# First layer of the later groups: 26 block products in four banks in place of 7 products in two

## The chip, the core and the metric

The kernel runs on one core of a Trainium2 chip. The metric is the device time of one execution in microseconds. The engines of the core are TensorE (in profiles PE for matmuls, PEld for its weight loads), VectorE (DVE), ScalarE (ACT), GpSimd (POOL) and SyncE (SP, which issues the transfers). Each engine works through its own list of instructions, and semaphores hold an instruction back until what it needs is there.

## The reference

An attention with decay (a "retention") over 4 batches, 8 heads, 768 positions and head size 64 gives x of 3072 tokens by 512. Two matmuls with an activation between them follow:

```python
def _moe_ref(x, w_in, w_out):
    h = x @ w_in                     # (3072, 512) @ (512, 2048)
    sp = np.maximum(h, 0.0) + np.log1p(np.exp(-np.abs(h)))
    g = h * erf(sp)
    return (g @ w_out).astype(np.float32)   # (3072, 2048) @ (2048, 512)
```

All is fp32 on the chip; the two weight matrices arrive as 64-bit floats and are converted on VectorE and ScalarE.

## The kernel before

The first 512 tokens go through plain matmuls while the weights are still being converted. The other 2560 tokens go in ten chunks of 256, and each chunk in two halves of the hidden columns (s = 0 and 1): 20 "later groups". In a later group both layers use Strassen's scheme in its form with seven products (Winograd): a 2x2 block product with sums of blocks takes 7 block products in place of 8. Here is the first layer:

```python
PRODUCTS = {
    1: ("11", "11"), 2: ("12", "21"), 3: ("S4", "22"), 4: ("22", "T4"),
    5: ("S1", "T1"), 6: ("S2", "T2"), 7: ("S3", "T3"),
}
...
def hidden_part(g, p):
    m, s = chunk_of(g), (g - G0) % 2
    ...
    a, b = PRODUCTS[p]
    if a[0] == "S":
        need("sums in", s)
    bank = BK[g][0 if p in (1, 6, 7, 4) else 1]
    for u in range(FG):                      # FG = 4
        for kk in range(2):
            nc.tensor.matmul(                # line 852
                bank[:, u, :],
                w_in_sb[:, s, IN[a], kk, u * P : (u + 1) * P],
                XS[m][b][:, kk, :],
                start=(p in (1, 2, 5) and u == 0 and kk == 0), stop=True, ...
            )
    pace(1.5)
    flat = bank.rearrange("p u t -> p (u t)")
    if p == 1:
        nc.scalar.copy(h["11"], flat)
    elif p == 2:
        nc.vector.tensor_tensor(h["11"], h["11"], flat, op=ALU.add)
    ...                                      # 4 copies and 3 additions in all, 128x512 each
```

So a group has 7 x 8 = 56 matmuls of 128x128x128. The sums S of the weights are made once per half by `sums`, four operations of 128x1024; the sums T of the inputs once per chunk by `x_sums`, four of 128x256. The order of a later group:

```python
for g in range(G0, NG):
    first = g == G0
    more = j < NJ
    hidden_part(g, 1)
    hidden_part(g, 2)
    if first:
        gated(g - 1)
    if put is not None:
        for step in range(3):
            put_part(put, step)
    hidden_part(g, 6)
    if first:
        sub_begin(j)
        sub_states(j)
    for _ in range(2):
        next(last_steps, None)
    ...
    if not first:
        g_sums(g - 1)
    hidden_part(g, 5)
    hidden_part(g, 7)
    for _ in range(2):
        next(last_steps, None)
    ...
        project_part(g - 1, 1)
    hidden_part(g, 4)
    hidden_part(g, 3)
    if more:
        sub_visit(j, g)                      # attention of one block of 128 positions
    if g + 1 < NG and (g - G0) % 2:
        x_sums(g + 1)
    if more:
        ... K_(j + 2); T(j + 2)              # scales and transposes on VectorE
    ...
        for p in (2, 4):
            project_part(g - 1, p)
        gate(g)                              # Softplus, then Erf, on ScalarE
        for p in (5, 6, 7, 3):
            project_part(g - 1, p)
    ...
        gated(g)                             # h * erf on VectorE, two of 128x1024
```

`last_steps` yields the sums for the second half of w_in and for w_out one operation at a time; `need` runs it until what is asked for is done. `project_part` is one product of the second layer (4 matmuls of 128x256), and ends with `next(last_steps, None)`; products 5, 6, 7 and 3 read the sums that `g_sums` makes, and 4 to 7 read sums of w_out ("T1" to "T4"). `put_part` adds the products of a chunk up to the output. PSUM has two banks from `ps_h` (hp), two from `ps_r` (r, also used by the attention) and four from `ps_o` (o).

The conversion of the weights uses scratch in places that are free early on: the parts of w_in_sb and w_out_sb that the sums will fill later.

Of the kernel before, what the change touches and what calls it, by code (L numbers as in the profile page):

```python
# [13 lines left out]
U32 = mybir.dt.uint32  # L14
# [18 lines left out]
IN = {"11": 0, "12": 1, "21": 2, "22": 3, "S3": 2, "S1": 4, "S2": 5, "S4": 6}  # L33
# [6 lines left out]


# [4 lines left out]
def kernel(  # L46
# [84 lines left out]
    w_in_sb = const.tile([P, 2, 7, 2, FG * P], F32, name="w_in_sb")  # L131
    w_out_sb = const.tile([P, 2, 7, FG, DH], F32, name="w_out_sb")

    def w_in_of(ft, kk):
        half, s, i = ft // (2 * FG), ft % (2 * FG) // FG, ft % FG
        return w_in_sb[:, s, 2 * half + kk // 2, kk % 2, i * P : (i + 1) * P]

    def w_out_of(ft):
# [6 lines left out]
    spare = [  # L145
        x[:, s, 4:7].rearrange("p a b c -> p (a b c)") for s, x in
        ((0, w_out_sb), (1, w_out_sb), (1, w_in_sb), (0, w_in_sb))
    ]
    raws = [x[:, : 2 * CE].bitcast(I64) for x in spare]
    numbers = spare[0][:, 2 * CE :].bitcast(U32)  # L150
    powers = [x[:, 2 * CE :].bitcast(U32) for x in spare[1:3]]
# [38 lines left out]
    def conversion(n):  # L190

        which, i = pieces[n]
        half, s, at = i // 4, i % 4 // 2, i % 2


        parts = itertools.product(
            range(2) if n < 4 else (None,), (slice(2), slice(2, 4)) if n == 0 else (slice(None),)
        )  # L200
        for part, rows in parts:
            last = n > 0 or rows.start == 2
            words = raws[place[n]].bitcast(U32)
            if which == "in":
                f = slice(at * 2 * P, (at + 1) * 2 * P)
                if part is not None:
                    f = slice((at * 2 + part) * P, (at * 2 + part + 1) * P)
                to = w_in_sb[:, s, 2 * half : 2 * half + 2, :, f].rearrange("p d k f -> p (d k) f")
            else:
                to = w_out_sb[:, s, 2 * half : 2 * half + 2, at * 2 : at * 2 + 2, :].rearrange(  # L210
                    "p d f c -> p d (f c)"
                )
            words = words.rearrange("p (a b w) -> p a b w", a=to.shape[1], w=2)
            number, power = (
                x.rearrange("p (a b) -> p a b", a=to.shape[1]) for x in (numbers, powers[n % 2])
            )
            if part is not None:
                f = slice(part * P, (part + 1) * P)
                words, number, power = words[:, rows, f], number[:, rows, f], power[:, rows, f]
                to = to[:, rows]  # L220
            lo, hi = words[:, :, :, 0], words[:, :, :, 1]
            nc.vector.tensor_scalar(power, hi, 0x7FF00000, None, op0=ALU.bitwise_and)
            nc.scalar.activation(power, power, AF.Relu, bias=below, scale=8.0)
            if part is None:
                yield
            nc.vector.tensor_scalar(
                number, hi, 0xFFFFF, 1 << 20, op0=ALU.bitwise_and, op1=ALU.bitwise_or
            )
            yield
            numberf = number.bitcast(F32)  # L230
            nc.vector.scalar_tensor_tensor(numberf, number, 2.0**32, lo, op0=ALU.mult, op1=ALU.add)
            if part is None:
                yield
            nc.vector.scalar_tensor_tensor(
                power, hi, 1 << 31, power, op0=ALU.bitwise_and, op1=ALU.bitwise_or
            )
            if part != 0 and last:
                load_pieces_after(n)
            yield
            nc.vector.scalar_tensor_tensor(  # L240
                to, numberf, 2.0**-52, power.bitcast(F32), op0=ALU.mult, op1=ALU.mult,
            )
            if last:
                done.update((which, 2 * i + u) for u in (range(2) if part is None else (part,)))
            yield

    def sums(which, s):

        if which == "in":
            assert all(("hidden", 2 * FG + s * FG + u) in done for u in range(FG))  # L250
            x = {name: w_in_sb[:, s, at] for name, at in IN.items()}
            of = (("S1", "21", "22", 1), ("S2", "S1", "11", 0), ("S3", "11", "21", 0), ("S4", "12", "S2", 0))
        else:
            assert ("project", s) in done
            x = {name: w_out_sb[:, s, at] for name, at in OUT.items()}
            of = (("T1", "12", "11", 0), ("T2", "22", "T1", 0), ("T3", "22", "12", 0), ("T4", "21", "T2", 0))
        for to, a, b, plus in of:
            nc.vector.tensor_tensor(x[to], x[a], x[b], op=ALU.add if plus else ALU.subtract)
            yield
        done.add(("sums " + which, s))  # L260
# [76 lines left out]
    state_1, state_2 = (const.tile([P, HP, D], F32, name=f"state{i}") for i in range(1, 3))  # L337
# [479 lines left out]
    XS, BK = {}, {}  # L817
# [6 lines left out]
    def x_quarter(m, dh, th):  # L824
        at = m % 2 * SCH + th * P
        return XC[m // 2][:, 2 * dh : 2 * dh + 2, at : at + P]

    def x_sums(g):

        m = chunk_of(g)  # L830
        xs = ret.tile([P, 4, 2, P], F32, name="xs", bufs=1)
        b11, b12, b21, b22 = (x_quarter(m, d, t) for d in range(2) for t in range(2))
        t1, t2, t3, t4 = (xs[:, i] for i in range(4))
        for to, a, b in ((t1, b12, b11), (t2, b22, t1), (t3, b22, b12), (t4, b21, t2)):
            nc.vector.tensor_tensor(to, a, b, op=ALU.subtract)
        XS[m] = {"11": b11, "21": b21, "22": b22, "T1": t1, "T2": t2, "T3": t3, "T4": t4}

    def hidden_part(g, p):


        m, s = chunk_of(g), (g - G0) % 2
        if p == 1:
            HS[g] = act.tile([P, N], F32, name="h")
            BK[g] = [ps_h.tile([P, FG, P], F32, name="hp") for _ in range(2)]
        h = {name: HS[g][:, i * TCH : (i + 1) * TCH] for name, i in HQ.items()}
        a, b = PRODUCTS[p]
        if a[0] == "S":
            need("sums in", s)
        bank = BK[g][0 if p in (1, 6, 7, 4) else 1]
        for u in range(FG):  # L850
            for kk in range(2):
                nc.tensor.matmul(  # L852
                    bank[:, u, :],
                    w_in_sb[:, s, IN[a], kk, u * P : (u + 1) * P],
                    XS[m][b][:, kk, :],
                    start=(p in (1, 2, 5) and u == 0 and kk == 0),
                    stop=True,
                    skip_group_check=True,
                )
        pace(1.5)  # L860
        flat = bank.rearrange("p u t -> p (u t)")
        if p == 1:
            nc.scalar.copy(h["11"], flat)
        elif p == 2:
            nc.vector.tensor_tensor(h["11"], h["11"], flat, op=ALU.add)  # L865
            pace(-0.6)
        elif p == 6:
            nc.scalar.copy(h["12"], flat)  # L868
        elif p == 7:
            nc.scalar.copy(h["22"], flat)  # L870
            other = BK[g][1].rearrange("p u t -> p (u t)")
            nc.vector.tensor_tensor(h["22"], h["22"], other, op=ALU.add)  # L872
            pace(-0.6)
        elif p == 4:
            nc.scalar.copy(h["21"], flat)  # L875
        elif p == 3:
            nc.vector.tensor_tensor(h["12"], h["12"], flat, op=ALU.add)  # L877
            pace(-0.6)
# [18 lines left out]
    def g_sums(g):  # L897
# [4 lines left out]
        for i in range(4):  # L902
            x[f"S{i + 1}"] = HS[g][:, i * TCH : (i + 1) * TCH]
        for to, a, b, plus in (
# [3 lines left out]
        G[g] = x  # L908
        pace(-2.4)
# [87 lines left out]
    def next_scores():  # L997
# [39 lines left out]
            ([], [(x_sums, G0)]),  # L1037
# [4 lines left out]
    for g in range(G0):  # L1042
# [10 lines left out]
        if g:  # L1053
            for tt in range(TT):
# [12 lines left out]
                elif g == G0 - 1 and tt == 1:  # L1067
                    load(JPC + 4)

    j = JPC + 2
    put = None
    for g in range(G0, NG):
        first = g == G0
        more = j < NJ
        hidden_part(g, 1)
        hidden_part(g, 2)
        if first:
            gated(g - 1)  # L1080
        if put is not None:
            for step in range(3):
                put_part(put, step)
        hidden_part(g, 6)
# [3 lines left out]
        for _ in range(2):  # L1088
            next(last_steps, None)
        if put is not None:  # L1090
            put_part(put, 3)
            put = None
        if not first:
            g_sums(g - 1)
        hidden_part(g, 5)
        hidden_part(g, 7)
        for _ in range(2):
            next(last_steps, None)
        if first:
            K_(j + 1)  # L1100
            T(j + 1)
            project(g - 1, 0)
        else:
            project_part(g - 1, 1)
        hidden_part(g, 4)
        hidden_part(g, 3)

# [17 lines left out]
        else:  # L1125
            for p in (2, 4):
                project_part(g - 1, p)
# [68 lines left out]
```

## Time and profile before

| | |
|---|---|
| time, median of 2 runs | 679.71 us (679.61 to 679.81) |
| span of the profiled execution | 677.6 us |
| TensorE busy | 671.8 us, 99% of the span |
| VectorE busy | 392.1 us, 58% |
| ScalarE busy | 257.0 us, 38% |
| mean granted TensorE clock | 1.000 |

Busy time is the time in which at least one instruction of the engine runs. In the list of groups a row has the line, the engine and operation, output and inputs with shapes, the count, the busy time and mean length of one, and the idle time of the engine just before such instructions with what ended it. Every fp32 matmul stands in the list as two records. A timeline row has the start in us from the span's start, the length, and the instruction; where rows overlap, operations are queued and the distance of their starts is what one of them costs.

### The profile page before, as it was taken

The page shows a single profiled execution, that of the slowest core. Times are in us where ns is not written, and L with a number is a line of the kernel's source. Part 1 is how long each engine was busy: PE and PEld are TensorE (multiplying, and loading weights), DVE is VectorE, ACT ScalarE, POOL GpSimd, SP SyncE. Part 2 cuts the span into 40 slices and gives each one's busy share as a digit, 9 for nine tenths or more (in the row PEclk, how much of TensorE's full clock was granted, in tenths as well). Part 3 has the DMA queues.
Part 4 walks back from the last instruction along what each step waited for, and adds up shares of the span by engine and source line. Part 5 has one row for each costly group of instructions (what it writes and reads, how often), then busy time and mean ns, then how long its engine had stood idle before and what let it go on. Part 6 is the DMA issues. An engine that isn't in the chain of part 4 may idle for free.

```text
span 677.6 us, 14849 instructions
## 1 busy us (share of the span) xinstructions
PE 671.8 (99%) x6400; PEld 575.4 (85%) x6400; DVE 392.1 (58%) x635; ACT 257.0 (38%) x294; POOL 7.4 (1%) x20
## 2 busy tenths in 40 slices
PE   8999999999999999999999999999999999999998
PEld 7744444668999999999999999999999999999997
DVE  5999999667845445634644553554554544333324
ACT  3477453333414415334144143242341441432430
POOL 1000000200000000000000000000000000000000
PEclk9999999999999999999999999999999999999999
DMA  9999753333423112312322321222222300000000
GB/s 188 231 254 256 178 144 77 59 61 62 119 48 75 34 32 47 76 36 43 76 41 38 76 46 31 64 44 47 69 40 45 74 2 1 1 33 1 1 32 31
DMA packets 156721, 47.67 MB, mean 70 GB/s; under 512 B 143088, under 2 KB 147568, under 8 KB 156656
## 3 DMA queue, kind: packets, MB, share of 16 engines
q1 hardware_dynamic: 156240, 46.72, 31.6%
q8 instruction: 50, 0.82, 0.5%
q14 instruction: 15, 0.12, 0.1%
q10 hardware_dynamic: 416, 0.01, 0.0%
HBM read 40.39 MB, written 6.29 MB: 69 GB/s over the span
## 4 chain that ended last, share of the span: by engine, by line
PE 98%; DMA 1%; DVE 0%; SPq 0%; ACT 0%; issue 0%
PE hp L852 37%; PE o L924 36%; PE hp L759 8%; PE o L795 8%; PE r L638 2%; PE hp L530 1%; PE o L674 1%; DMA kq<-in_k_dram 1%; PE hp L653 1%; PE r L459 1%; PE r L653 1%; PE o L506 1%; PE r L446 1%; PE r L674 0%; PE o L515 0%; PE o L499 0%
## 5 line engine op out<-in xcount | busy, mean ns | idle before, releaser
L852 PE MATMUL hp<-xs,w_in_sb 128*128 128x128 f32 x1280 | 149.7, 275 | 0.0
L852 PEld LDWEIGHTS hp<-xs,w_in_sb 128*128 128x128 f32 x1280 | 147.8, 192 | 1.5 <-issue 0.5
L924 PE MATMUL o<-w_out_sb,h 128*128 128x256 f32 (+1 forms) x648 | 142.0, 377 | 0.4 <-DVE r L1151 0.4
L924 PEld LDWEIGHTS o<-w_out_sb,h 128*128 128x128 f32 x648 | 122.3, 190 | 16.8 <-DVE r L1151 0.6
L852 PE MATMUL hp<-xT,w_in_sb 128*128 128x128 f32 x960 | 113.7, 275 | 0.0
L852 PEld LDWEIGHTS hp<-xT,w_in_sb 128*128 128x128 f32 x960 | 112.0, 192 | 1.9 <-issue 1.0
L924 PE MATMUL o<-w_out_sb,e 128*128 128x256 f32 x480 | 112.1, 383 | 0.0
L748 DVE TENSOR_TENSOR e<-h,e 128x1024 f32<-128x1024 f32 x42 | 49.5, 1221 | 100.0 <-ACT e L729 100.0
L924 PEld LDWEIGHTS o<-w_out_sb,e 128*128 128x128 f32 x480 | 88.3, 190 | 11.4
L759 PE MATMUL hp<-xT,w_in_sb 128*128 128x512 f32 (+2 forms) x144 | 56.5, 548 | 0.0
L877 DVE TENSOR_TENSOR h<-h,hp 128x512 f32<-128x512 f32 x20 | 13.8, 688 | 72.3 <-PE hp L852 72.3
L719 ACT ACT_TABLE_LOAD x24 | 30.8, 1283 | 60.8 <-issue 45.4
L759 PEld LDWEIGHTS hp<-xT,w_in_sb 128*128 128x128 f32 x144 | 25.8, 190 | 26.9 <-issue 24.6
L729 ACT ACTIVATE e<-e 128x2048 f32<-128x2048 f32 (+1 forms) x23 | 42.1, 1836 | 0.2
L719 ACT ACTIVATE e<-h 128x2048 f32<-128x2048 f32 x22 | 42.0, 1910 | 0.2
L865 DVE TENSOR_TENSOR h<-h,hp 128x512 f32<-128x512 f32 x20 | 13.7, 687 | 37.5 <-PE hp L852 37.5
L870 ACT COPY h<-hp 128x512 f32<-128x512 f32 x20 | 11.7, 586 | 61.0 <-PE hp L852 61.0
L875 ACT COPY h<-hp 128x512 f32<-128x512 f32 x20 | 11.7, 585 | 60.3 <-PE hp L852 60.3
L868 ACT COPY h<-hp 128x512 f32<-128x512 f32 x20 | 11.7, 585 | 57.1 <-PE hp L852 57.1
L692 ACT COPY xT<-r 128x256 f32<-128x256 f32 x33 | 10.8, 375 | 57.9 <-PE r L638 57.9
L729 ACT ACT_TABLE_LOAD x24 | 30.8, 1283 | 0.4
L872 DVE TENSOR_TENSOR h<-h,hp 128x512 f32<-128x512 f32 x20 | 13.8, 688 | 27.8 <-ACT h L870 27.8
(144 smaller groups left out, 667.8 us busy)
## 6 DMA issues: line engine op xcount, KB each, us to landing
w_out_sb<-in_moe_w_out_dram SPq DMA_DIRECT2D x14, 512.0 KB, 5.5
kq<-in_k_dram SPq DMA_DIRECT2D x23, 256.0 KB, 3.9
v<-in_v_dram SPq DMA_DIRECT2D x23, 256.0 KB, 3.2
out_dram<-r SPq DMA_DIRECT2D x23, 256.0 KB, 2.7
kq<-in_q_dram SPq DMA_DIRECT2D x288, 16.0 KB, 1.8
kb<-in_k_dram SPq DMA_DIRECT2D x288, 16.0 KB, 1.7
w_in_sb<-in_moe_w_in_dram SPq DMA_DIRECT2D x8, 512.0 KB, 9.5
w_in_sb<-in_moe_w_in_dram SPq DMA_DIRECT2D x8, 256.0 KB, 7.7
```

The source lines that it names most:

```text
L638: nc.tensor.matmul(pp[r][col * D : (col + 1) * D, u % 2, t], x[own, u, :], QT[j][own, u, t], start=first(r, col), stop=True, skip_group_ch ...
L653: nc.tensor.matmul(other[a][own, u % 2, D:] if crossed else pp[a][own, u % 2, t], V[j][t, 2 * u + r, :], AM[j][t, r, u, :D], start=crossed ...
L719: nc.scalar.activation(E[g], HS[g], AF.Softplus)
L729: nc.scalar.activation(E[g][:, half], E[g][:, half], AF.Erf)
L748: nc.vector.tensor_tensor(E[g][:, half], HS[g][:, half], E[g][:, half], op=ALU.mult)
L759: nc.tensor.matmul(HP_[ft][:, t], w_in_of(ft, kk), XC[0][:, kk, t], start=(kk == 0), stop=(kk == n_k - 1),)
L795: nc.tensor.matmul(O[0][tt].rearrange("p (d c) -> p d c", d=2), E[g][:, u * TCH + tt * P : u * TCH + (tt + 1) * P], w_out_of(ft), start=(f ...
L852: nc.tensor.matmul(bank[:, u, :], w_in_sb[:, s, IN[a], kk, u * P : (u + 1) * P], XS[m][b][:, kk, :], start=(p in (1, 2, 5) and u == 0 and ...
L865: nc.vector.tensor_tensor(h["11"], h["11"], flat, op=ALU.add)
L872: nc.vector.tensor_tensor(h["22"], h["22"], other, op=ALU.add)
L877: nc.vector.tensor_tensor(h["12"], h["12"], flat, op=ALU.add)
L924: nc.tensor.matmul(O[m][i][:, half, at], G[g][a][:, u * P : (u + 1) * P], w_out_sb[:, s, OUT[b], u, at], start=i not in started, stop=(s = ...
```

## The change

The first layer of a later group is cut finer: 4x4 blocks of weights times 4x2 blocks of inputs, 26 block products in place of 28 (7 products of 4 blocks each). Each product ("step") is two matmuls of 128x128x128 for 256 hidden columns. The steps are spread over four banks, two hp and two r. In each bank they form chains: a step mostly adds to what is there, and the running sum is read after the step, sometimes by two readers. The first read of each of the 8 blocks of h is a copy on ScalarE, the others are additions or subtractions on VectorE. The aim is fewer matmuls.

It needs other sums: 30 of the weights per half (128x256 each, many in place), 18 of the inputs per chunk (128x128 each). w_in_sb is laid out in 26 blocks, and the conversion's scratch moves: one part into the tile xs of the inputs' sums, one into a slice of w_out_sb; the state of the attention's third block goes into a buffer of kb. The core of the diff:

```diff
+N_W, N_X = 26, 18
+W_SUMS = (
+    (16, 2, 6, "+"),
+    (17, 8, 10, "-"),
+    ...                                      # 30 in all: target, operands, sign
+)
+X_SUMS = (
+    (0, (1, 0), (1, 1), "-"),
+    ...                                      # 18 in all
+)
+STEPS = (                                    # weight, input, bank, starts the chain, reads
+    (21, (1, 0), 0, True, ((4, True),)),
+    (20, 5, 1, True, ((1, False),)),
+    (10, 14, 2, True, ((3, True),)),
+    (22, 0, 3, True, ((5, True),)),
+    (23, 7, 0, False, ((5, True),)),
+    (24, (0, 1), 1, False, ((7, False),)),
+    (25, 15, 2, False, ((2, True),)),
+    (14, (2, 1), 3, False, ((7, True),)),
+    (9, 8, 0, False, ((7, True),)),
+    (12, 6, 1, False, ((6, False),)),
+    (2, 11, 2, True, ((2, False), (6, True))),
+    (17, 1, 3, True, ((2, False), (4, True))),
+    (15, 10, 0, False, ((6, True),)),
+    ...                                      # 26 in all
+)
...
-    w_in_sb = const.tile([P, 2, 7, 2, FG * P], F32, name="w_in_sb")
+    w_in_sb = const.tile([P, 2, N_W, 2 * P], F32, name="w_in_sb")
...
-    powers = [x[:, 2 * CE :].bitcast(U32) for x in spare[1:3]]
+    later = ret.tile([P, N_X, P], F32, name="xs", bufs=1)[:, : CE // P].rearrange("p a f -> p (a f)")
+    powers = [halves(spare[1][:, 2 * CE :]), halves(later)]
+    last_power = halves(spare[1][:, :CE])
...
+    def sum_in(s, upto):
+        while in_sums[s] < upto:
+            to, a, b, sign = (x if i == 3 else w_in_sb[:, s, x] for i, x in enumerate(W_SUMS[in_sums[s]]))
+            nc.vector.tensor_tensor(to, a, b, op=OP[sign])
+            in_sums[s] += 1
...
     def sums(which, s):
         if which == "in":
+            for n in range(4, 17, 4):
+                sum_in(s, n)
+                yield
+            return
...
-    def hidden_part(g, p):
+    def hidden_steps(g):
+        banks = [pool.tile([P, FG, P], F32, name=name) for pool, name in ((ps_h, "hp"), (ps_r, "r")) for _ in range(2)]
+        for w, x, bank, first, reads in STEPS:
+            sum_in(s, max([n for n, of in enumerate(W_SUMS, start=1) if of[0] == w], default=0))
+            to = banks[bank]
+            for u in range(2):
+                nc.tensor.matmul(
+                    to[:, u, :],
+                    w_in_sb[:, s, w, u * P : (u + 1) * P],
+                    XS[m](x),
+                    start=first and u == 0,
+                    ...
+            of = to[:, :2].rearrange("p u t -> p (u t)")
+            for o, plus in reads:
+                h = h_block(g, o)
+                if o in written:
+                    nc.vector.tensor_tensor(h, h, of, op=ALU.add if plus else ALU.subtract)
+                elif plus:
+                    nc.scalar.copy(h, of)
+                else:
+                    nc.scalar.activation(h, of, AF.Copy, scale=-1.0)
+                written.add(o)
+            yield
```

The order of a later group becomes:

```diff
-        hidden_part(g, 1)
-        hidden_part(g, 2)
...
-        for _ in range(2):
-            next(last_steps, None)
...
         if first:
             sub_begin(j)
             sub_states(j)
+        elif put is not None:
+            put_part(put, 0)
+        more_sums = iter(()) if first else g_sums(g - 1)
+        for n, _ in enumerate(hidden_steps(g), start=1):
+            if first:
+                if n == 2:
+                    gated(g - 1)
+                elif n == 14:
+                    K_(j + 1)
+                    T(j + 1)
+                    project(g - 1, 0)
+                continue
+            if n in (4, 5, 8) and put is not None:
+                put_part(put, {4: 1, 5: 2, 8: 3}[n])
+            if n in (13, 14, 15, 16):
+                next(more_sums)
+            if n in (14, 18, 24):
+                project_part(g - 1, {14: 1, 18: 2, 24: 4}[n])
...
-            for p in (2, 4):
-                project_part(g - 1, p)
             gate(g)
             for p in (5, 6, 7, 3):
                 project_part(g - 1, p)
```

Both calls of `next(last_steps, None)` outside `project_part` are gone, and the first `x_sums` moves behind the end of the conversion.

## The prediction

> **What bounds the kernel now.** I read the engines' busy shares first, then the chain that ended last, then the costliest groups of instructions.
>
> ```profile
> PE 671.8 (99%) x6400; PEld 575.4 (85%) x6400; DVE 392.1 (58%) x635; ACT 257.0 (38%) x294; POOL 7.4 (1%) x20
> ...
> PE 98%; DMA 1%; DVE 0%; SPq 0%; ACT 0%; issue 0%
> PE hp L852 37%; PE o L924 36%; PE hp L759 8%; PE o L795 8%; PE r L638 2%; PE hp L530 1%; PE o L674 1%; DMA kq<-in_k_dram 1%; PE hp L653 1%; PE r L459 1%; PE r L653 1%; PE o L506 1%; PE r L446 1%; PE r L674 0%; PE o L515 0%; PE o L499 0%
> ...
> L852 PE MATMUL hp<-xs,w_in_sb 128*128 128x128 f32 x1280 | 149.7, 275 | 0.0
> L852 PE MATMUL hp<-xT,w_in_sb 128*128 128x128 f32 x960 | 113.7, 275 | 0.0
> L877 DVE TENSOR_TENSOR h<-h,hp 128x512 f32<-128x512 f32 x20 | 13.8, 688 | 72.3 <-PE hp L852 72.3
> ```
>
> TensorE is the bound, with 98% of the chain; L852, the first layer of the 20 later groups, is 37% of it and has no idle time in front. VectorE waits for TensorE (72.3 us at L877 alone). So TensorE work taken out of L852 is worth its full time only while VectorE stays ahead. That makes VectorE's order the question, so I read its timeline around the end of one group (226 to 238 us):
>
> ```profile
> 227.75 0.53 DVE L694 TENSOR_TENSOR xT<-xT,hp 128x128 f32<-128x128 f32 x2
> 228.20 0.41 DVE L699 TENSOR_TENSOR state<-state,r 128x256 f32<-128x256 f32 x1
> 228.53 0.42 DVE L835 TENSOR_TENSOR xs<-xT 128x256 f32<-128x256 f32 x1
> 228.98 0.43 DVE L835 TENSOR_TENSOR xs<-xT,xs 128x256 f32<-128x256 f32 x1
> 229.32 0.42 DVE L835 TENSOR_TENSOR xs<-xT 128x256 f32<-128x256 f32 x1
> 229.66 0.42 DVE L835 TENSOR_TENSOR xs<-xT,xs 128x256 f32<-128x256 f32 x1
> 229.99 0.69 DVE L417 TENSOR_TENSOR kq<-kq,kq_s 128x512 f32<-128x512 f32 x1
> ...
> 232.43 0.67 DVE L439 STREAM_TRANSPOSE qT<-kq 128x512 f32<-128x512 f32 x1
> 237.44 2.36 DVE L748 TENSOR_TENSOR e<-h,e 128x1024 f32<-128x1024 f32 x2 [4.35 <-ACT e L729]
> ```
>
> Starts give the spacing of queued operations: 0.34 us for 128x256 (229.32 to 229.66), 0.46 where one reads what the one before wrote (228.53 to 228.98), so 0.12 more; 0.60 for 128x512. An L607 pair of 128x128 took 0.48 us with 0.28 for one, so 0.20 each. The last line is the gate's product: after a wait of 4.35 us for ScalarE it begins at 237.44, just before TensorE's next group at 237.66. Last, the windows of the first two later groups:
>
> ```profile
> 127.50:157.10 29.60, 29.60 (x289) 21.52 (x288) 17.80 (x27) 9.44 (x11) 0.00 (x0) 1.00 0.36 66
> 157.10:184.00 26.90, 26.90 (x297) 25.30 (x296) 22.00 (x33) 11.33 (x14) 0.00 (x0) 1.00 0.37 87
> ```
>
> The columns are length, then busy time of PE, PEld, DVE, ACT. In the second, 22.0 of 26.9 us of VectorE are already taken.
>
> [...] So a step that writes a bank waits until the read of its last step there is over, even if it only accumulates. The trace before shows one such wait, at the end: 0.38 us before TensorE for VectorE's L1151. [...] The timeline agrees as far as it goes: everything runs in program order. [...] the trace has 688 and 1221 ns for 128x512 and 128x1024, a difference of 533.
>
> **Part 1, products removed.** 7 products x 8 matmuls = 56 per group become 26 x 2 = 52. Each matmul is two records; 80 records of a group took 344.81 to 353.75 us, 0.112 us each. Four matmuls are 8 x 0.112 = 0.89 us, times 20 groups: **-17.9 us**. A step is 4 records, 0.447 us.
>
> **Part 2, reads of the banks.** Per group ScalarE's 4 copies of 0.585 us become 8 of about 0.375 (as L692); VectorE's 3 additions of 0.69 become 18 of 0.42. A step in the same bank usually comes four steps later, that is 1.8 us. In the build's VectorE order the gate's product of the group before stands ahead of the first read. Step 9 needs the read of step 5; without a wait it starts 8 x 0.447 = 3.6 us after step 1.
> - In a group after an even one, the times of before hold: from the end of the hidden steps ScalarE needs 2.8 us to its last copy of xT and 6.46 for tables, Softplus and Erf; the product takes 2.36, together 11.65. TensorE has 2.0 for the attention and 32 x 0.216 = 6.9 for four projection parts, 8.9. So the product ends 2.75 after step 1 begins. One addition of the output (0.6) goes first, then the read (0.42) and 0.15 to wake TensorE: 3.9, a wait of 0.3. More output additions before the reads of steps 8 and 9 make step 13 wait 0.5. Together **0.8 us**, 9 groups (3, 5, to 19): +7.2.
> - In a group after an odd one, 18 sums of inputs stand ahead of the product in place of 4: 18 x 0.2 plus about 0.6 for dependences, 4.2 us for 1.5. With 3.4 before (attention) and 3.05 after (scales and transposes, 5 x 0.6) the product starts at 10.65 instead of 9.3, ends 4.0 after step 1, and step 9 waits **0.95 us**, 7 groups (4 to 16): +6.6.
>
> So in the steady part the waits, about 0.85 us a group, eat almost all of the 0.89 saved.
>
> **Part 3, sums of the weights, once.** Four 128x1024 sums per half (4.75 us) become 30 of 128x256. For the first half 16 are done early, 14 inside group 0; for the second half all 30 are inside group 1, because the calls that spread them were removed. They stand in VectorE's queue between reads: n sums just after the last read make TensorE wait 0.2 (from TensorE to VectorE) + 0.34 for the read + 0.34(n-1) + 0.42 + 0.15, 0.12 more per dependence.
> - Group 0: VectorE ended its transposes at 126.25; 16 early sums instead of four cost 1.3 more and the input sums 2.7 more, then three small operations and the product: 133.6. Step 1 starts near 128.65 (127.46 plus 1.2 for the scores, now ahead of it), so step 9 waits 1.7. Step 10 waits 1.4, step 13 with two sums 2.0, steps 16 and 17 0.4, step 21 with five sums 2.6, 25 and 26 2.3. Sum **10.4**.
> - Group 1: nine sums after the gate's product, 9 x 0.34 plus dependences = 3.8, less 0.7 of lead: step 1 waits 3.1. Step 6 (two) 1.45, 10 (three) 1.8, 13 2.0, 16 and 17 1.5, 21 2.6, 26 1.6. Projection part 4 needs four sums of w_out (1.2 each) that are now issued right there: 0.2 + 0.34 + 4.7 + 0.15 = 5.4. Sum **19.4**.
> - Group 2: two more w_out sums (2.35) stand ahead of its gate product, which ends 6.4 after step 1; step 9 waits **3.3**.
>
> **Sum.** -17.9 + 7.2 + 6.6 + 10.4 + 19.4 + 3.3 = +29.0, less what I may count twice where one wait absorbs the next (about 1): 679.7 + 28 = **708 us**.
>
> **Rivals.** (a) The saving comes through whole: reads are short and VectorE has 42% of the span idle. Then 679.7 - 17.9 = 662. Against it: the idle share is an average, and groups 0 and 1 are nearly full before anything is added. (b) VectorE only has to be fast enough in sum. Group 1 then has 2.36 + 11.3 (30 sums) + 6.1 (18 reads) + 2.5 + 7.0 = 29.3 us of VectorE from a start 3 us before step 1, against 16.8 us of hidden steps and three parts: about 10 us of loss, group 0 about 5, and the steady waits vanish: 679.7 - 17.9 + 17 = 679. Against it: a read in the queue ahead of a sum waits for TensorE, which waits for the sum, so they take turns. (c) The new scratch places for the conversion delay the start: few operations and the same sizes move, under 1 us.
>
> **Range and chances.** The one-off waits (33 us) follow from order and measured durations; I allow a third less. The steady waits may halve, or grow by a restart of about 0.1 us each. That gives 692 to 720. To be within 2% the one-off waits would have to be half of mine; to be over 2% faster nearly all waits must be absent. Faster 0.03, within 2% 0.12, slower 0.85.
>
> **What would show it.** In the profile after: 2080 records at the hidden line with an idle column of tens of us ended by VectorE, where it was 0.0; group 1 about 45 us long, group 0 about 38; later pairs of groups about 53.6 us, as before. The largest single waits: before projection part 4 and step 1 in group 1. Wrong if TensorE has no idle time at the hidden steps (then rival a), or if groups 0 and 1 lose under 17 us together (then rival b).

## The result and the profile after

The changed kernel takes 714.43 us (714.37 to 714.5), the kernel before 679.71: a ratio of 1.051, 95% interval 1.047 to 1.056. It is slower by 34.7 us. The 17.9 us of saved matmuls are there, but waits and a lower TensorE clock (0.983 on average, 1.000 before) took three times as much, 52.6 us, over three quarters of it in the first three later groups.

The page of the changed kernel, the lines that answer to those shown of before. The second and third line are the busy share of TensorE and its granted clock in 40 slices of the span:

```profile
PE 673.4 (95%) x6240; PEld 567.9 (80%) x6240; DVE 522.9 (73%) x1127; ACT 270.4 (38%) x374; POOL 7.8 (1%) x20
...
PE   8999999777758999999999999999999999999998
...
PEclk9999999999889999999999999999999999999999
...
PE 65%; DVE 22%; issue 5%; SPq 5%; DMA 2%; ACT 2%; DVEq 0%; ACTq 0%
...
L957 PE MATMUL hp<-xs,w_in_sb 128*128 128x128 f32 x1040 | 152.2, 282 | 15.0 <-DVE h L969 8.0
...
L969 DVE TENSOR_TENSOR h<-h,hp 128x256 f32<-128x256 f32 x200 | 83.8, 419 | 91.1 <-PE hp L957 89.8
...
L1021 PE MATMUL o<-w_out_sb,e 128*128 128x256 f32 x480 | 116.3, 386 | 5.2 <-DVE w_out_sb L358 5.2
```

L957 is the new line of the hidden matmuls, with 15.0 us of idle time in front where L852 had 0.0. TensorE has 160 records fewer (6240 for 6400), and yet is busy 1.6 us longer and idle far more: the chain that ends last went from 98% on TensorE to 65%, with 22% on VectorE. The dip in the busy row covers slices 8 to 13, from 125 to 231 us; the rest is as full as before. Most of it lies in the first two later groups, whose windows are (length, busy time of PE, PEld, DVE, ACT, POOL, then the clock):

```profile
128.50:172.00 43.50, 31.56 (x261) 21.31 (x253) 31.18 (x72) 12.16 (x19) 0.00 (x0) 0.95 0.29 52
172.00:220.00 48.00, 34.01 (x291) 30.19 (x292) 31.87 (x77) 10.04 (x14) 0.00 (x0) 0.83 0.15 40
```

They were 29.6 and 26.9 us long. VectorE, the engine that is waited for, is itself busy only 31 to 32 us of 43.5 and 48: the two engines take turns. The waits of TensorE by releaser, as total, times and longest, give the same:

```profile
PE hp L957 <- DVE w_in_sb L345: 11.0, 8, 1.9
PE hp L957 <- DVE h L969: 8.0, 18, 2.7
PE o L1021 <- DVE w_out_sb L358: 5.2, 1, 5.2
PE r L957 <- DVE w_in_sb L345: 4.9, 2, 2.4
PE hp L957 <- ACT r L912: 2.9, 1, 2.9
```

L345 are the sums of w_in, L358 those of w_out, L969 VectorE's reads of the banks. The last row names ScalarE, but the timeline shows that VectorE was the one that came last. First TensorE in the second later group, then VectorE (start, length, instruction, idle time before it):

```profile
171.97 1.19 PE L957 MATMUL hp<-xT,w_in_sb 128*128 128x128 f32 x4 [2.95 <-ACT r L912]
...
196.86 1.16 PE L957 MATMUL r<-xT,w_in_sb 128*128 128x128 f32 x8 [2.44 <-DVE w_in_sb L345]
...
204.09 3.78 PE L1021 MATMUL o<-w_out_sb,e 128*128 128x256 f32 x8 [5.18 <-DVE w_out_sb L358]
```

```profile
168.04 4.85 DVE L345 TENSOR_TENSOR w_in_sb<-w_in_sb 128x256 f32<-128x256 f32 x12
...
194.02 0.87 DVE L969 TENSOR_TENSOR h<-h,hp 128x256 f32<-128x256 f32 x2 [1.68 <-PE hp L957]
194.80 2.01 DVE L345 TENSOR_TENSOR w_in_sb<-w_in_sb 128x256 f32<-128x256 f32 x5
...
199.29 7.14 DVE L358 TENSOR_TENSOR w_out_sb<-w_out_sb 128x1024 f32<-128x1024 f32 x6
```

The middle rows show the pattern. VectorE sits idle 1.68 us for TensorE, because a read stands first in its queue; only then come five sums, 2.01 us, and TensorE sits idle 2.44 us for them. The first sums of the group (nine ahead of step 1 and three for later steps) are one block of twelve from 168.04; TensorE starts before the block has ended, at 171.97, when the ninth is done (171.76; ScalarE's L912 had ended at 171.11).

Where the time went, by the start of each later group on TensorE (the first of them called group 0): group 0 is 13.3 us longer than before, group 1 20.8, group 2 3.6; the start of group 0 is 1.6 later, mostly because the scores now stand ahead of it; and the last 17 groups together are 4.6 shorter. The sum is +34.7. Counted this way, the wait of 2.95 us ahead of group 1's first step stands in group 0.

### The profile page after: what moved, and what is told of

Read it like the earlier page. It is cut to its first block, busy times and chain, and to the rows that moved or that the text cites. A ratio compares the mean times of both kernels' runs of the same rounds, so it can differ in the third digit from the quotient of the medians.

```text
span 712.3 us, 15308 instructions
## 1 busy us (share of the span) xinstructions
PE 673.4 (95%) x6240; PEld 567.9 (80%) x6240; DVE 522.9 (73%) x1127; ACT 270.4 (38%) x374; POOL 7.8 (1%) x20
## 4 chain that ended last, share of the span: by engine, by line
PE 65%; DVE 22%; issue 5%; SPq 5%; DMA 2%; ACT 2%; DVEq 0%; ACTq 0%
PE o L1021 27%; PE hp L957 21%; PE r L957 9%; SPq L187 4%; DVE xs L938 3%; PE o L897 2%; DVE e L850 2%; DVE h L969 2%; DVE w_in_sb L345 1%; PE r L740 1%; DMA kq<-in_q_dram 1%; DVE w_out_sb L317 1%; DVE w_out_sb L325 1%; DVE w_out_sb L358 1%; PE o L776 1%
## 5 line engine op out<-in xcount | busy, mean ns | idle before, releaser
L957 PE MATMUL hp<-xs,w_in_sb 128*128 128x128 f32 x1040 | 152.2, 282 | 15.0 <-DVE h L969 8.0
L957 PEld LDWEIGHTS hp<-xs,w_in_sb 128*128 128x128 f32 x1040 | 137.9, 195 | 23.6 <-DVE h L969 11.4
L969 DVE TENSOR_TENSOR h<-h,hp 128x256 f32<-128x256 f32 x200 | 83.8, 419 | 91.1 <-PE hp L957 89.8
L969 DVE TENSOR_TENSOR h<-h,r 128x256 f32<-128x256 f32 x160 | 61.9, 418 | 15.4 <-PE r L957 13.0
L957 PE MATMUL r<-xs,w_in_sb 128*128 128x128 f32 x480 | 69.2, 282 | 1.4 <-DVE am L639 1.4
L957 PEld LDWEIGHTS r<-xs,w_in_sb 128*128 128x128 f32 x480 | 62.5, 197 | 1.7 <-issue 1.6
L971 ACT COPY h<-hp 128x256 f32<-128x256 f32 x40 | 14.9, 372 | 109.2 <-PE hp L957 76.8
L957 PE MATMUL hp<-xT,w_in_sb 128*128 128x128 f32 x320 | 49.7, 278 | 6.9 <-DVE w_in_sb L345 4.0
L957 PEld LDWEIGHTS hp<-xT,w_in_sb 128*128 128x128 f32 x320 | 43.9, 193 | 9.3 <-ACT r L912 3.7
L861 PEld LDWEIGHTS hp<-xT,w_in_sb 128*128 128x128 f32 x144 | 25.7, 190 | 27.0 <-issue 24.6
L973 ACT ACTIVATE h<-hp 128x256 f32<-128x256 f32 x60 | 23.0, 383 | 46.9 <-PE hp L957 45.4
L957 PE MATMUL r<-xT,w_in_sb 128*128 128x128 f32 x240 | 33.5, 276 | 4.9 <-DVE w_in_sb L345 4.9
```

Of the source, the lines that this page charges most:

```text
L861: nc.tensor.matmul(HP_[ft][:, t], w_in_of(ft, kk), XC[0][:, kk, t], start=(kk == 0), stop=(kk == n_k - 1),)
L957: nc.tensor.matmul(to[:, u, :], w_in_sb[:, s, w, u * P : (u + 1) * P], XS[m](x), start=first and u == 0, stop=True, skip_group_check=True,)
L969: nc.vector.tensor_tensor(h, h, of, op=ALU.add if plus else ALU.subtract)
L971: nc.scalar.copy(h, of)
L973: nc.scalar.activation(h, of, AF.Copy, scale=-1.0)
```

## The experiments

All times are medians beside the kernel before on the same chip (679.4 to 679.6 us). In the expectations, a letter stands for what the text beside it says. My theory from the prediction, A, is that the order of VectorE's queue makes the waits: one-off sums between reads, and reads behind other work in the steady part.

**1. Sums of w_in left out.** The last 14 sums of the first half and all 30 of the second aren't made; their blocks hold zeros or older values, so the output isn't the reference's. TensorE's work is the same.

```diff
-            nc.vector.tensor_tensor(to, a, b, op=OP[sign])
+            if s == 0 and in_sums[s] < 16:
+                nc.vector.tensor_tensor(to, a, b, op=OP[sign])
```

> The changed kernel with the last 14 weight sums of the first half and all 30 of the second left out (zeros or older values stand in their place). Theory A (reads and sums take turns in VectorE's queue, and TensorE waits in each turn): the waits put down to the weight sums, 11.0 + 4.9 us, and the one of 2.9 us before the first step of group 1 go, and with them some 6 us of slow TensorE clock after waits: 714.4 - 25 = about 689 us. Rival B (only VectorE's throughput counts): at most its 44 operations of 0.38 us, 17 us: 697 us or more. Rival C (the 18 reads per group are the bound by themselves, the sums are hidden): 705 us or more.

Measured: 686.96 us, ratio 1.011 (1.009 to 1.013). So 27.5 us came from these sums. Of TensorE's waits, the rows of L345 and the 2.9 are gone (18.8 us), and those of L969 and w_out stay:

```profile
PE hp L958 <- DVE h L970: 7.9, 18, 2.7
PE o L1022 <- DVE w_out_sb L359: 5.2, 1, 5.2
```

(All lines are one further down here.) Most of the 8.7 us beyond the idle time is the clock, whose mean over the span rose from 0.983 to 0.994: TensorE's busy time in stretches at half clock fell from 19.3 us to 6.8, and half of the difference is 6.2 (an estimate).

**2. The same sums on GpSimd.** All are computed, 44 of w_in and 8 of w_out (the last four at the end of group 0), by an engine that was idle.

```diff
-            nc.vector.tensor_tensor(to, a, b, op=OP[sign])
+            engine.tensor_tensor(to, a, b, op=OP[sign])
...
+    sum_in(0, len(W_SUMS), nc.gpsimd)
+    sum_in(1, len(W_SUMS), nc.gpsimd)
+    for _ in sums("out", 0, nc.gpsimd):
+        pass
```

> The changed kernel with the last 14 sums of the first half, all 30 of the second and the eight sums of w_out on GpSimd, issued before the later groups. Theory A: beside what the run without weight sums gains, the wait of 5.2 us before projection part 4, most of the 2.7 us of group 2 and some 3 us of slow clock go: 678 to 681 us, TensorE's mean clock back at 1.00. Rival: GpSimd takes over 1.5 us per sum or holds VectorE up, TensorE then waits for GpSimd in groups 0 and 1: 695 us or more.

Measured: 692.35 us, ratio 1.019 (1.017 to 1.021). Faster than the changed kernel by 22 us, but 11 over what I expected. The timelines of GpSimd and VectorE of this run show why:

```profile
124.31 38.32 POOL L345 TENSOR_TENSOR w_in_sb<-w_in_sb 128x256 f32<-128x256 f32 x44
162.60 21.85 POOL L358 TENSOR_TENSOR w_out_sb<-w_out_sb 128x1024 f32<-128x1024 f32 x8
```

```profile
163.83 5.50 DVE L850 TENSOR_TENSOR e<-h,e 128x1024 f32<-128x1024 f32 x2 [2.06 <-ACT e L831]
...
176.66 0.41 DVE L969 TENSOR_TENSOR h<-h,hp 128x256 f32<-128x256 f32 x1
176.99 2.51 DVE L1005 TENSOR_TENSOR h<-h,e 128x512 f32<-128x512 f32 x1
179.42 2.83 DVE L1005 TENSOR_TENSOR h<-e 128x512 f32<-128x512 f32 x1
```

While GpSimd adds, VectorE's gate product takes 5.50 us in place of 2.36, and the four 128x512 additions of L1005, on SBUF tiles alone, 2.00 to 2.83 in place of 0.69. The reads L969, which have one input in PSUM, keep their length: the 28 from 119 to 185 us, all but the last beside GpSimd, took 413 ns (hp) and 418 ns (r) on average. Why was not shown; 2.8 us is close to the mean of one GpSimd sum of 128x1024 (2.73 us). The largest waits of TensorE became 7.2 us for the first mask of group 0, which stands behind 18 sums of inputs, and 4.9 for a read. That the sums off VectorE's queue help holds; that GpSimd's time is free falls.

**3. Scales and transposes later.** From the third later group on, K_ and T of the next attention block are issued after steps 18 and 24 in place of the group's end, so that they don't stand ahead of the gate's product.

```diff
+            if n == 18 and g > G0 + 1 and j + 1 < NJ:
+                K_(j + 1)
+            if n == 24 and g > G0 + 1 and j + 1 < NJ:
+                T(j + 1)
...
-            if j + 2 < NJ:
+            if j + 2 < NJ and first:
```

> The changed kernel with the scales of keys and queries and their transposes (5 operations, 3.05 us) moved from ahead of the gate's product to steps 18 and 24 of the next group, from group 2 on. Theory A (step 9 waits because the gate's product stands late in VectorE's queue after the 18 input sums): the wait of 0.46 us in even groups goes (7 groups, 3.2 us), and the 2.7 us of group 2 with 1 to 2 us of slow clock: 714.4 - 7 = about 707 us. Rival D (the reads are late by themselves): no change, 713 to 715 us.

Measured: 708.2 us, ratio 1.042 (1.041 to 1.044). TensorE's waits for L969 fall from 8.0 us to 2.5. In the steady part a group after an odd one takes 25.92 us (380.92 to 406.84) where the changed kernel takes 26.64 (382.73 to 409.37). Five of the seven such groups gain 0.72 us and two gain 0.52, and the last 17 groups together 4.8. Group 2 is 4.5 shorter. Against that the profiled run (709.4 us) reached group 2 4.0 us later than the changed kernel, with nearly the same waits in groups 0 and 1. By estimate the clock accounts for it: its mean was 0.978 for 0.983, there were seven stretches at half clock for five, and half of TensorE's busy time in them is 13.4 us for 9.6. So the net gain of 6.2 is not made of the moved operations alone.

**4. Sums of w_out earlier.** The four sums of the first half of w_out are issued at the end of group 0, not ahead of projection part 4 in group 1. Three more calls of `next(last_steps, None)` after that part keep the other half's sums where they were.

```diff
-        for which, n in (("in", 1), ("out", 0), ("out", 1)):
+        for which, n in (("in", 1), ("out", 1)):
...
+            for _ in sums("out", 0):
+                pass
```

> The changed kernel with the four w_out sums of the first half issued at the end of group 0, behind the scales and transposes, and not right before projection part 4 of group 1. Theory A: the wait of 5.2 us and some 2 us of slow clock behind it go; VectorE has about 3 us free there, so the rest of the 4.7 us delays step 1 of group 1 by 1.6 us: 714.4 - 5.6 = about 709 us. Rival (the wait only moves to the front of group 1): 713 to 715 us.

Measured: 708.82 us, ratio 1.044 (1.042 to 1.045), 5.6 less than the changed kernel. The wait of 5.2 is gone, and step 1 of group 1 waits 4.4 in place of 2.9, since it now has those sums ahead of it.

**5. All one-off sums left out, scales later.** Runs 1, 3 and the remaining sums together. 44 sums of w_in and all 8 of w_out are left out (zeros or older values in their place; the output isn't the reference's).

> The changed kernel with all one-off sums on VectorE left out (44 of w_in, 8 of w_out; the blocks that they fill hold zeros, so the output is not the reference's), and with the scales and transposes of kq moved to steps 18 and 24 from the third later group on. Theory A (the fewer matmuls are worth their 17.9 us, and only waits for VectorE, one-off and steady, hide it): 679.7 - 17.9 = 661.8, plus what is left of steady waits, about 0.3 us a group = 5, so 667, at the most 671. If the separate gains only add up (714.4 less 27.4, 6.3 and 5.5): 675. Theory B (the finer chains cost TensorE something in themselves, more banks, more records beginning a chain, so the 0.112 us a record isn't reached): 676 or more, with the mean length of a record or the idle time at the hidden line showing it.

Measured: 671.01 us, ratio 0.987 (0.986 to 0.989), clock 1.000. The first three later groups take 82.7 us together, where the kernel before takes 83.4 and the changed kernel 121.1. TensorE does the same 6240 records as in the changed kernel and needs 43 us less; queued records still start 0.112 us apart. So the finer chains cost TensorE next to nothing in themselves.

**6. Plain products in the first two later groups.** The whole computation. Groups 0 and 1 need no sums this way, and VectorE makes the one-off sums, those of w_out too, beside their 64 matmuls and at the end of group 2. The scales come later as in run 3, and the 16 sums made during the conversion move as well.

```diff
-        for n, _ in enumerate(hidden_steps(g), start=1):
+        second = g == G0 + 1
+        for n, _ in enumerate((plain_steps if first or second else hidden_steps)(g), start=1):
...
+            if second:
+                if n == 1:
+                    sum_in(0, 30)
...
+        if first:
+            sum_in(0, 18)
+        elif second:
+            sum_in(1, 15)
+        elif g == G0 + 2:
+            sum_in(1, 30)
```

> The whole computation. The first two later groups, one of each half of the weights, use plain products (64 matmuls of 128x128x128 and four copies on ScalarE each, no sums), and VectorE makes the one-off sums of the weights in their time and at the end of the third group; the scales and transposes are moved as in the run before. Theory A: 18 groups save 0.89 us each, 16.1; the two plain ones cost 8 matmuls of 0.224 us more than before each, 3.6; steady waits 0.3 us a group, 5: 679.7 - 16.1 + 3.6 + 5 = 672, faster than both kernels by about 1%. If the sums still hold up TensorE by one wait of 2 to 4 us in each of the three groups: 680. Theory B (chains dear in themselves): 682 or more.

Measured: 672.9 us, ratio 0.990 (0.989 to 0.992), as expected and faster than both kernels. What is left shows in the steady part, TensorE and then VectorE:

```profile
374.26 1.16 PE L960 MATMUL hp<-xs,w_in_sb 128*128 128x128 f32 x8
375.26 1.10 PE L960 MATMUL r<-xs,w_in_sb 128*128 128x128 f32 x8
376.58 1.16 PE L960 MATMUL hp<-xs,w_in_sb 128*128 128x128 f32 x8 [0.22 <-DVE h L972]
```

```profile
370.92 2.36 DVE L849 TENSOR_TENSOR e<-h,e 128x1024 f32<-128x1024 f32 x2 [5.82 <-ACT e L830]
373.20 0.69 DVE L1069 TENSOR_TENSOR r<-o,r 128x512 f32<-128x512 f32 x1
373.80 0.41 DVE L972 TENSOR_TENSOR h<-h,hp 128x256 f32<-128x256 f32 x1
```

The read of step 5 stands behind an output addition (L1069) that nothing needs yet, and the two reads after it likewise.

**7 and 8. Output additions later**, on top of runs 6 and 5 (run 8 leaves out what run 5 does):

```diff
-            if n in (4, 5, 8) and put is not None:
-                put_part(put, {4: 1, 5: 2, 8: 3}[n])
+            if n in (5, 6, 9) and put is not None:
+                put_part(put, {5: 1, 6: 2, 9: 3}[n])
```

> The kernel with plain products in the first two later groups, with one more change: the additions of the output (steps 1 to 3 of put_part) are issued after steps 5, 6 and 9 in place of 4, 5 and 8, so that the reads of steps 5 and 9 stand ahead of them in VectorE's queue. In the trace of the run before, step 9 started about 0.1 us late and step 12 and 13 about 0.5 together, 0.63 us in every group that writes an output, nine of them. Theory A (the order of VectorE's queue alone makes the steady waits): up to 9 x 0.63 = 5.7 us less, 667 to 669. Theory C (VectorE has too much to do there in any order, the wait only moves to another step or to the first projection part): 672 to 673 as before.

> The kernel with all one-off sums left out (its output is not the reference's) and the scales moved, with the additions of the output issued after steps 5, 6 and 9 as in the run beside it. Theory A: 671.0 less up to 5.7 = 665.3, within 4 us of the full saving, 679.7 - 17.9 = 661.8. Theory C: 671 as before.

Measured: 670.36 us for run 7 (ratio 0.987, 0.985 to 0.989), 668.68 for run 8 (0.984, 0.983 to 0.986). Each gained about 2.5 us, under half of what I expected at best, because step 12 now waits 0.28 us: the read of step 8 stood behind both additions of the output's second step. Run 8 stays about 7 us above the full saving, not within 4: of this 3.4 us lie in the last 17 groups and 3.2 ahead of them, where the mask of group 0 still costs 1.4.

**9. The second addition of that step later still**, on top of run 7:

```diff
         elif step == 2:
             ...
-            nc.vector.tensor_tensor(r[:, 3], r[:, 6], o57[:, 0], op=ALU.add)
+            if m == chunk_of(NG - 1):
+                nc.vector.tensor_tensor(r[:, 3], r[:, 6], o57[:, 0], op=ALU.add)
         else:
+            nc.vector.tensor_tensor(r[:, 3], r[:, 6], o57[:, 0], op=ALU.add)
             nc.vector.tensor_tensor(r[:, 1:3], r[:, 5:7], o34, op=ALU.add)
```

> The run before this (670.4 us) left one wait: step 12 started about 0.28 us late, with a slower record after it, 0.36 us in every group that writes an output, because the read of step 8 stood behind both additions of the output's second step. Here the second of these (r[:, 3], 128x256) is issued with the third step instead, after the read of step 9. Theory A (order of the queue alone): step 12 no longer waits, 9 x 0.36 = 3.2 us less, 667.2. Theory C (the wait moves to step 15, 16 or the first projection part): 670.

Measured: **667.79 us**, ratio 0.983 (0.981 to 0.985), the whole computation. From its page:

```profile
PE 659.8 (99%) x6288; PEld 561.9 (84%) x6288; DVE 502.6 (75%) x1073; ACT 269.0 (40%) x366; POOL 5.0 (1%) x20
...
PE 98%; DMA 1%; DVE 0%; ACT 0%; SPq 0%; issue 0%
...
L960 PE MATMUL hp<-xs,w_in_sb 128*128 128x128 f32 x936 | 131.6, 276 | 0.0
```

The idle time in front of the hidden matmuls is 0.0 again and the chain is 98% TensorE, as in the kernel before. Most of the later groups take 25.92 or 26.02 us where before they took 26.81. Counting matmuls alone gives, as an estimate, 679.4 - 18 x 0.894 + 2 x 8 x 0.2235 = 666.9. VectorE still has 110 us more work than before (502.6 for 392.1), and it costs under 1 us. In the 18 groups that keep the finer scheme it was the order of VectorE's work that counted, not its amount.

## Why the prediction was right, step by step

The prediction was 708.0, the measurement is 714.4. The direction and the mechanism held; terms of the sum were off in both directions, and one cost was missing.

- **Part 1, products removed: right.** 24 queued records of the changed kernel took 2.68 us (368.30 to 370.98), 0.112 each. Run 9 comes within 0.9 us of the time that follows from counting matmuls alone.
- **Part 2, steady waits: right in kind, too large by a quarter.** A group without waits takes 26.81 - 0.89 = 25.92 us, and that is what runs 3 and 9 show. In the changed kernel most groups after an odd one take 26.64, a loss of 0.72 (predicted 0.95, where the prediction's own terms put the end of the product 4.1 after step 1 and not 4.0, which gives 1.1), those after an even one 26.55 to 26.68, 0.63 to 0.76 (predicted 0.8; run 9 takes 0.53 to 0.66 off such groups). The last 17 groups lost 10.6 us (17 x 0.894 - 4.6) in place of 13.8. A pair takes 53.2 us; I had said 53.6. Runs 3, 7 and 9 removed these waits by moving the very operations that the prediction had placed ahead of the reads. That a step which only adds to its bank waits for the read there shows at step 9 (0.46 us for L969, up to 386.92).
- **Part 3, group 1: right.** The waits predicted, and in brackets those measured: step 1 3.1 (2.95), step 6 1.45 (1.34), 10 1.8 (1.88), 13 2.0 (1.64), 16 and 17 1.5 (0.20), 21 2.6 (2.44), part 4 5.4 (5.18), 26 1.6 (1.31); sum 19.4 (16.9). Only steps 16 and 17 are mis-sized: their sums found VectorE free among the sums of the gate (L1005). The 0.2 and 0.15 us reckoned between the engines fit the end of the kernel before: VectorE's L1151 (673.30) starts 0.05 us after TensorE's modelled end, itself 0.16 past the next possible start, and TensorE's next record (673.64) 0.05 after VectorE's end, with 1.16 us for eight records in place of 1.05.
- **Part 3, group 0: sum right, one wait in another place.** 10.4 (9.0). Steps 10, 13 and 21 waited 1.40, 1.92 and 2.44 (1.4, 2.0, 2.6). But the 1.7 put down to step 9 came at step 3 as 1.4: its r bank still held scores, and the mask that reads them (L639) stood behind the 18 sums of inputs.
- **Group 2:** 3.3 (2.7).
- **The missing term: TensorE's clock.** In five stretches, each after a wait, the changed kernel's TensorE ran at half clock. Two of them, each with the stretch ahead of it, and between them a stretch that no drop followed; last, the steady part (length, busy time of PE and so on; the clock is the third figure from the end):

```profile
137.24:140.65 3.41, 1.49 (x14) 1.29 (x13) 2.17 (x6) 0.38 (x1) 0.00 (x0) 1.00 0.78 151
140.65:144.06 3.41, 3.41 (x10) 1.86 (x9) 2.81 (x6) 0.00 (x0) 0.00 (x0) 0.50 0.22 34
...
147.47:150.89 3.42, 1.54 (x14) 1.35 (x13) 3.02 (x8) 0.17 (x1) 0.00 (x0) 1.00 0.23 36
...
198.67:202.09 3.42, 0.25 (x3) 0.05 (x1) 3.10 (x4) 0.00 (x0) 0.00 (x0) 1.00 0.00 0
202.09:208.91 6.82, 4.64 (x12) 3.63 (x12) 4.45 (x5) 0.00 (x0) 0.00 (x0) 0.50 0.00 0
...
371.50:424.70 53.20, 52.52 (x577) 48.77 (x576) 39.11 (x93) 20.35 (x29) 0.00 (x0) 1.00 0.25 51
```

  Projection part 4 took 3.78 us after its wait, where such a part takes 1.89. The other three stretches at 0.50 are 171.37 to 174.78, 181.61 to 188.43 and 225.98 to 229.39. Half of PE's busy time in the five is 9.6 us: 1.7 in group 0, 6.3 in group 1, 1.6 in group 2. That is an estimate, but run 1's clock rose to 0.994 when those waits went, and runs 5, 6 and 9, without them, ran at 1.000, runs 6 and 9 with the whole computation. Counted with the wait ahead of its first step, group 0 took 40.0 us and group 1 50.7, where I had said about 38 and 45.
- **Sum.** -17.9 + 10.6 + 28.6 (9.0, 16.9 and 2.7 of waits) + 9.6 (clock) = 30.9. Idle time in the trace starts at a record's modelled end, 0.16 us after the next could start (0.61 for four records spaced 0.447), so 15 waits are 2.4 us more: 33.3. Of the other 1.4 of the 34.7, 0.5 is group 0's later start beyond the moved scores; the rest I can't place. That the total came so near is partly luck: the predicted waits were 7.7 us too long (46.9 for 39.2), which made up for most of a cost that the prediction lacked.
- **Rivals.** (a), the saving whole, needs the waits gone: not in this kernel, but nearly so in run 9. (b), only VectorE's total counts, falls: in the windows of groups 0 and 1 both engines have idle time, and run 9, with 96% of the changed kernel's busy time on VectorE, loses next to nothing. (c), the conversion's scratch: group 0 starts 1.6 us later, of which the scores that moved ahead of it are 1.1; what is left is under 1, as I had said. That part wasn't tried by itself.

## What to carry to other kernels

A change that trades matmuls for vector operations must be priced where each operation stands in the queue: an addition of 0.34 us ahead of a read of a bank holds up the matmuls that wait for the bank, while over 100 us of the same work in idle places cost less than 1 us. Put the reads that free a bank first and work that nothing waits for behind them, and spread one-off preparation over a stretch that doesn't need it yet, even if that stretch then does more matmuls. If TensorE must wait, count its slower records after the wait too (here an estimated 9.6 us beside 39.2 us of waits).

## What the runs showed of the hardware

In the changed kernel short waits went ahead of half clock. Every stretch at half clock is 3.41 us long or twice that, and the starts of the five lie whole multiples of 3.413 us apart (140.65, 171.37, 181.61, 202.09 and 225.98: nine, three, six and seven of them), so the whole trace is read here in stretches of that length. In the stretch ahead of each of the five TensorE was idle for 1.92, 2.35, 1.88, 3.17 and 2.53 us, and each ended after 3.41 us in which it was idle for 0.6 us at the most. From full clock, no stretch with less idle time led to a drop in this kernel (the most was 1.87 us, between 147.47 and 150.89). That is no sharp limit: in run 3 one drop followed a stretch with about 1.7 us, and idle time rests on modelled ends. How a wait fell on these stretches went with the outcome too. The wait of step 21 in group 0 was 2.44 us long in the changed kernel, where the end of a stretch at 150.89 fell inside it and no drop followed, and as long in run 3, where by the lengths of the records it lay within one stretch and half clock followed.

A GpSimd sum of 128x256 fp32 took 861 ns on average and one of 128x1024 2733 in run 2, with VectorE at work beside it. VectorE's queued ones stand 0.34 us (229.32 to 229.66 before) and 1.2 us apart (six of w_out in 7.14 us in the changed kernel). In run 2 VectorE's operations on SBUF tiles alone took up to four times as long beside GpSimd's sums (2.83 us for 0.69, L1005), those with an input in PSUM as long as without (0.41 to 0.42 us, L969).
